# Linear attention, RMS norm and phase token mixing on one core: another token order, packed remainders, and the norm's root on another engine

## The chip, the core and the metric

The kernel runs on one core of a Trainium2 chip. A core has engines that run side by side and wait for each other through semaphores: TensorE (PE; its weight loads are listed apart as PEld), VectorE (DVE), ScalarE (ACT), GpSimd (POOL) and SyncE (SP), which here only issues transfers. In both kernels TensorE writes its results to tiles in the memory PSUM, of which the pool `psA` holds eight. The metric is the time of one execution on the device in microseconds (us), lower is better, as a median of several runs.

## What is computed

Eight batches, eight heads of 64 channels, 576 tokens. Linear attention without softmax is followed by an RMS norm per token and head; the heads side by side give x of 576 x 512 per batch. A phase theta = x·w_theta turns x into two parts, which two token matrices mix over the 576 tokens. A channel product with ReLU ends it.

```python
kv = np.einsum('bhsd,bhse->bhde', k, v)
out = np.einsum('bhsd,bhde->bhse', q, kv)
rms = np.sqrt(np.mean(out * out, axis=-1, keepdims=True) + 1e-06)
x = out / rms * g_norm                   # then (B, S, H*D)
theta = x @ w_theta
zr = x * np.cos(theta)
zi = x * np.sin(theta)
y = np.einsum('ts,bsd->btd', w_tok_r, zr) + np.einsum('ts,bsd->btd', w_tok_i, zi)
u = x + y
result = u + np.maximum(u @ w_ch, 0.0)
```

576 tokens are four tiles of 128 and a remainder of 64. Inputs and output are fp32; after the attention product the kernel works in fp16 with fp32 sums.

## The kernel before

P is 128, C 512, S 576, D 64, NT 5 (token tiles, the last of 64), NKC 4 (channel blocks). Per batch: `attention` loads q, k and v in runs of one token of one head (64 fp32 values, 256 bytes), forms k·v for each pair of heads in fp32 and keeps its two diagonal blocks, transposes q, forms raw = q·kv, and normalises raw tile by tile: squares on ScalarE, sums on VectorE, the power -1/2 on GpSimd (line 186), the product with g_norm (line 190) and with raw (line 197) on VectorE. k is loaded by GpSimd's own queue. `moe_head` transposes x, forms theta, reduces it to one turn (lines 234 to 251), and takes sine and cosine on ScalarE. `moe_mid` mixes over tokens; its output has tokens on the partitions. `moe_tail2` transposes u, multiplies by w_ch and stores. The code is set four columns to the left here; cuts are marked `# ...`.

```python
def attention(b):
    # ...
    for (dst, src, eng) in ((qt, q, nc.sync), (kt, k, nc.gpsimd), (vt, v, nc.sync)):
        for h in range(H):
            eng.dma_start(
                out=dst[:, 0:NT - 1, h, :],
                in_=src[b, h, 0:(NT - 1) * P, :].rearrange(
                    "(sc p) d -> p sc d", p=P
                ),
            )
    # ...
    for hp in range(NHP):
        kvps = psA.tile([P, P], FP32, tag="psA", name=f"kvps{b}_{hp}")
        for sc in range(NT):
            nc.tensor.matmul(
                kvps[:, :],
                kt[:tsz[sc], sc, 2 * hp:2 * hp + 2, :],
                vt[:tsz[sc], sc, 2 * hp:2 * hp + 2, :],
                start=(sc == 0),
                stop=(sc == NT - 1),
            )
        # ...
        nc.vector.memset(kbd[:], 0.0)
        nc.scalar.copy(kbd[0:64, 0:64], kvps[0:64, 0:64])
        nc.scalar.copy(kbd[64:128, 64:128], kvps[64:128, 64:128])
            # ...
            nc.tensor.matmul(
                dst_ap,
                qt[:tsz[sc], sc, 2 * hp:2 * hp + 2, :],
                ident[:tsz[sc], :tsz[sc]],
                is_transpose=True,
                start=(sc in (0, NT - 1)),
            # ...
            )
    # ...
    for ti in range(NT):
        n = tsz[ti]
        raw = psA.tile([P, C], FP32, tag="psA", name=f"raw{b}_{ti}")
        for hp in range(4):
            nc.tensor.matmul(
                raw[:n, hp * P:(hp + 1) * P],
                qT_pair[hp][:, ti * P:ti * P + n],
                kv_bd[hp][:],
                start=(hp == 0),
                stop=(hp == 3),
            )
        # ...
        nc.scalar.activation(out=sq[:n, :], in_=raw[:n, :], func=AFT.Square)
        # ...
        nc.vector.reduce_sum(
            out=sst[:n, :], in_=sq[:n, :].rearrange("p (h e) -> p h e", h=H),
            axis=mybir.AxisListType.X,
        )
        # ...
        nc.gpsimd.tensor_tensor(
            out=rt[:n, :], in0=sse[:n, :], in1=mhalf[:n, 0:H], op=ALU.pow
        )
        # ...
        nc.vector.tensor_tensor(
            out=gr[:n, :].rearrange("p (h e) -> p h e", h=H),
            in0=g_rep[:n, :].unsqueeze(1).broadcast_to((n, H, D)),
            in1=rt[:n, :].unsqueeze(2).broadcast_to((n, H, D)),
            op=ALU.mult,
        )
        # ...
        nc.vector.tensor_tensor(
            out=x16[:n, :], in0=raw[:n, :], in1=gr[:n, :], op=ALU.mult
        )
# ...
def moe_head(b):
    # ...
    for kc in range(NKC):
        xps = psA.tile([P, S], FP16, tag="psA", name=f"xTps{b}_{kc}")
        for ti in range(NT):
            nc.tensor.matmul(
                xps[:, ti * P:ti * P + tsz[ti]],
                xb[ti][:tsz[ti], kc * P:(kc + 1) * P],
                ident16[:tsz[ti], :tsz[ti]],
                is_transpose=True,
            # ...
            )
        # ...
        nc.scalar.copy(out=t[:], in_=xps[:])
    # ...
    for ti in range(NT):
        n = tsz[ti]
        thps = psA.tile([P, C], FP32, tag="psA", name=f"th{b}_{ti}")
        for kc in range(NKC):
            nc.tensor.matmul(
                thps[:n, :],
                xT[kc][:, ti * P:ti * P + n],
                wth_t[kc][:],
                start=(kc == 0),
                stop=(kc == NKC - 1),
            )
        pt = work.tile([P, C], FP32, tag="pt", bufs=3, name=f"pt{b}_{ti}")
        nc.vector.tensor_scalar(
            out=pt[:n, :], in0=thps[:n, :], scalar1=INV2PI, scalar2=MAGIC,
            op0=ALU.mult, op1=ALU.add,
        )
        # ...
        nc.vector.tensor_scalar(
            out=mt[:n, :], in0=pt[:n, :], scalar1=MAGIC, scalar2=TWO_PI,
            op0=ALU.subtract, op1=ALU.mult,
        )
        # ...
        nc.vector.tensor_tensor(
            out=red[:n, :], in0=thps[:n, :], in1=mt[:n, :], op=ALU.subtract
        )
        # ...
        nc.vector.tensor_scalar(
            out=ared[:n, :].bitcast(I32), in0=red[:n, :].bitcast(I32),
            scalar1=0x7FFFFFFF, scalar2=None, op0=ALU.bitwise_and,
        )
        # ...
        nc.scalar.activation(
            out=sin_t[:n, :], in_=red[:n, :], func=AFT.Sin, scale=SIN_SHRINK
        )
        # ...
        nc.scalar.activation(
            out=cos_t[:n, :], in_=ared[:n, :], func=AFT.Sin,
            bias=pio2_t[:n], scale=-SIN_SHRINK,
        )
        # ...
        nc.vector.tensor_tensor(
            out=zrt[:n, :], in0=xb[ti][:n, :], in1=cos_t[:n, :], op=ALU.mult
        )
        # ...
        nc.vector.tensor_tensor(
            out=zit[:n, :], in0=xb[ti][:n, :], in1=sin_t[:n, :], op=ALU.mult
        )
# ...
def moe_mid(b):
    # ...
    for ti in range(NT):
        # ...
        for sc in range(NT):
            for (wT, zz) in ((wrT, zr), (wiT, zi)):
                nc.tensor.matmul(
                    yps[:n, :],
                    wT[sc][:tsz[sc], ti * P:ti * P + n],
                    zz[sc][:tsz[sc], :],
                    start=(i_mm == 0),
                    stop=(i_mm == n_mm - 1),
                )
        # ...
        nc.vector.tensor_tensor(
            out=ut[:n, :], in0=xb[ti][:n, :], in1=yps[:n, :], op=ALU.add
        )
# ...
def moe_tail2(b):
    # ...
    for kc in range(NKC):
        ups = psA.tile([P, S], FP16, tag="psA", name=f"uTps{b}_{kc}")
        for ti in range(NT):
            nc.tensor.matmul(
                ups[:, ti * P:ti * P + tsz[ti]],
                ub[ti][:tsz[ti], kc * P:(kc + 1) * P],
            # ...
            )
        # ...
        nc.scalar.copy(out=t[:], in_=ups[:])
    # ...
    for ti in range(NT):
        # ...
        for kc in range(NKC):
            nc.tensor.matmul(
                vps[:n, :],
                uT[kc][:, ti * P:ti * P + n],
                wch_t[kc][:],
                start=(kc == 0),
                stop=(kc == NKC - 1),
            )
        # ...
        nc.vector.scalar_tensor_tensor(
            out=ot[:n, :], in0=vps[:n, :], scalar=0.0, in1=ub[ti][:n, :],
            op0=ALU.max, op1=ALU.add,
        )
        nc.sync.dma_start(out=out[b, ti * P:ti * P + n, :], in_=ot[:n, :])
# ...
attention(0)
moe_head(0)
for b in range(1, B):
    attention(b)
    moe_mid(b - 1)
    moe_head(b)
    moe_tail2(b - 1)
moe_mid(B - 1)
moe_tail2(B - 1)
```

Ahead of this the weights are loaded: w_theta and w_ch in fp32 with a cast on ScalarE, the token matrices in fp32, transposed on TensorE and cast on the way out of PSUM. The order of instructions on an engine can differ from the program's where they do not depend on each other.

## Time and profile before

| | |
|---|---|
| median of three runs | 407.88 us (404.64 to 407.97) |
| span of the profiled execution | 404.0 us |
| instructions | 5022 |
| bytes read / written | 33.10 MB / 9.44 MB |
| mean granted TensorE clock | 0.916 |

In the lines of the profile, L186 is line 186 of the kernel; out<-in are the names of the tiles (written, then read), x40 the count, then the busy time in us and the mean duration of one in ns, and after a second bar the idle time of the engine just before such instructions, with what ended it. The clock row cuts the span into 40 slices; each digit is the clock granted to TensorE in tenths, 9 being 90% or more. The chain of waits is followed back from the last instruction, each step to what released it.

### The profile page before, as it was taken

The page shows a single profiled execution, that of the slowest core. Times are in us where ns is not written, and L with a number is a line of the kernel's source. Part 1 is how long each engine was busy: PE and PEld are TensorE (multiplying, and loading weights), DVE is VectorE, ACT ScalarE, POOL GpSimd, SP SyncE. Part 2 cuts the span into 40 slices and gives each one's busy share as a digit, 9 for nine tenths or more (in the row PEclk, how much of TensorE's full clock was granted, in tenths as well). Part 3 has the DMA queues.
Part 4 walks back from the last instruction along what each step waited for, and adds up shares of the span by engine and source line. Part 5 has one row for each costly group of instructions (what it writes and reads, how often), then busy time and mean ns, then how long its engine had stood idle before and what let it go on. Part 6 is the DMA issues. An engine that isn't in the chain of part 4 may idle for free.

```text
span 404.0 us, 5022 instructions
## 1 busy us (share of the span) xinstructions
PE 321.1 (79%) x1730; PEld 165.2 (41%) x1730; DVE 235.7 (58%) x515; ACT 156.9 (39%) x342; POOL 120.0 (30%) x120
## 2 busy tenths in 40 slices
PE   0258914997789958996989868995899689978894
PEld 0125701652347323642456324732374235524331
DVE  1000063867695659656694659565875777476953
ACT  2143513470276125540475027612553145503701
POOL 8500292076002920086005710291003400250000
PEclk9999955899699988999899969997999988996998
DMA  7999999069103960289006920398030001200033
GB/s 218 241 242 231 203 222 172 2 135 200 18 0 131 225 113 2 98 175 183 15 34 184 209 44 0 134 218 118 2 114 6 1 0 41 78 0 2 0 118 118
DMA packets 87369, 42.87 MB, mean 106 GB/s; under 512 B 78256, under 2 KB 78256, under 8 KB 87344
## 3 DMA queue, kind: packets, MB, share of 16 engines
q1 hardware_dynamic: 83888, 33.11, 40.0%
q0 software_dynamic: 3456, 9.44, 10.1%
q8 instruction: 14, 0.23, 0.3%
q14 instruction: 11, 0.09, 0.1%
HBM read 33.10 MB, written 9.44 MB: 105 GB/s over the span
## 4 chain that ended last, share of the span: by engine, by line
PE 37%; POOL 20%; DVE 18%; ACT 10%; DMA 7%; issue 5%; POOLq 1%; SPq 0%; DVEq 0%
POOL rt L186 15%; PE kvps L130 11%; PE th L226 9%; POOL k L114 6%; PE v L320 4%; DMA wths<-in_moe_w_theta_dram 4%; PE qTpsa L148 3%; DVE x L197 3%; DVE gr L190 3%; ACT uT L314 3%; ACT sin L253 3%; PE y L284 3%; DVE pt L234 2%; PE xTps L209 2%; ACT cos L257 2%
## 5 line engine op out<-in xcount | busy, mean ns | idle before, releaser
L114 POOL DMA_DIRECT2D k<-in_k_dram x64 | 48.3, 760 | 158.0 <-PE kvps L130 155.3
L186 POOL TENSOR_TENSOR rt<-sse,mhalf 128x8 f32<-128x8 f32 (+1 forms) x40 | 65.3, 1642 | 83.5 <-DVE sse L181 83.3
L284 PE MATMUL y<-zr,wrT 128*128 128x512 f16 (+3 forms) x200 | 76.6, 384 | 1.1 <-DVE x L197 1.1
L284 PE MATMUL y<-zi,wiT 128*128 128x512 f16 (+3 forms) x200 | 75.7, 379 | 0.0
L218 ACT COPY xT<-xTps 128x576 f16<-128x576 f16 x32 | 18.4, 651 | 110.0 <-PE xTps L209 109.8
L209 PE MATMUL xTps<-ident,x 128*128 128x128 f16 (+1 forms) x160 | 19.8, 250 | 41.4 <-DVE x L197 39.8
L130 PE MATMUL kvps<-v,k 128*128 128x128 f32 (+1 forms) x320 | 51.3, 299 | 1.6 <-ACT kvbd L140 1.6
L226 PE MATMUL th<-wth,xT 128*128 128x512 f16 (+1 forms) x160 | 51.4, 490 | 1.1 <-ACT xT L218 1.1
L190 DVE TENSOR_TENSOR gr<-g_rep,rt 128x512 f32<-128x512 f32 (+1 forms) x40 | 27.6, 691 | 41.1 <-POOL rt L186 41.1
L320 PE MATMUL v<-wch,uT 128*128 128x512 f16 (+1 forms) x160 | 41.4, 406 | 8.4 <-ACT uT L314 8.4
L130 PEld LDWEIGHTS kvps<-v,k 128*128 128x128 f32 (+1 forms) x320 | 41.4, 194 | 10.4 <-issue 2.9
L253 ACT ACTIVATE sin<-red 128x512 f16<-128x512 f32 (+1 forms) x40 | 25.2, 631 | 51.0 <-DVE red L244 51.0
L234 DVE TENSOR_SCALAR pt<-th 128x512 f32<-128x512 f32 (+1 forms) x40 | 26.6, 683 | 29.9 <-PE th L226 29.9
L138 DVE MEMSET kvbd<- 128x64 uint32 x32 | 3.1, 112 | 62.1 <-ACT qT L158 48.0
L284 PEld LDWEIGHTS <-wrT 128*128 128x128 f16 (+3 forms) x200 | 19.7, 98 | 44.3 <-issue 27.9
L209 PEld LDWEIGHTS <-x 128*128 128x128 f16 (+1 forms) x160 | 11.6, 109 | 51.5 <-DVE x L197 44.2
L328 DVE SCALAR_TENSOR_TENSOR ot<-v,u 128x512 f32<-128x512 f32 (+1 forms) x40 | 26.1, 679 | 9.9 <-DMA out_dram<-ot 6.8
L176 DVE TENSOR_REDUCE sst<-sq 128x8 f32<-128x512 f16 (+1 forms) x40 | 26.1, 679 | 8.4 <-ACT sq L174 8.0
L226 PEld LDWEIGHTS <-xT 128*128 128x128 f16 (+1 forms) x160 | 18.4, 123 | 31.0 <-issue 20.0
L257 ACT ACTIVATE cos<-ared,pio_t 128x512 f16<-128x512 f32 (+1 forms) x40 | 28.6, 718 | 0.7 <-DVE ared L248 0.4
L293 DVE TENSOR_TENSOR u<-x,y 128x512 f16<-128x512 f16 (+1 forms) x40 | 26.1, 672 | 3.5 <-PE y L284 3.4
L320 PEld LDWEIGHTS <-uT 128*128 128x128 f16 (+1 forms) x160 | 14.5, 105 | 31.9 <-ACT uT L314 15.6
(48 smaller groups left out, 367.2 us busy)
## 6 DMA issues: line engine op xcount, KB each, us to landing
k<-in_k_dram POOLq DMA_DIRECT2D x72, 128.0 KB, 5.8
q<-in_q_dram SPq DMA_DIRECT2D x72, 128.0 KB, 5.3
v<-in_v_dram SPq DMA_DIRECT2D x72, 128.0 KB, 4.9
out_dram<-ot SPq DMA_DIRECT2D x32, 256.0 KB, 2.0
wrnat<-in_moe_w_tok_r_dram SPq DMA_DIRECT2D x4, 288.0 KB, 7.4
winat<-in_moe_w_tok_i_dram SPq DMA_DIRECT2D x4, 288.0 KB, 4.0
wths<-in_moe_w_theta_dram SPq DMA_DIRECT2D x4, 256.0 KB, 7.0
wchs<-in_moe_w_ch_dram SPq DMA_DIRECT2D x4, 256.0 KB, 4.9
```

Source lines behind the costliest of these rows:

```text
L114: eng.dma_start(out=dst[:, 0:NT - 1, h, :], in_=src[b, h, 0:(NT - 1) * P, :].rearrange("(sc p) d -> p sc d", p=P),)
L130: nc.tensor.matmul(kvps[:, :], kt[:tsz[sc], sc, 2 * hp:2 * hp + 2, :], vt[:tsz[sc], sc, 2 * hp:2 * hp + 2, :], start=(sc == 0), stop=(sc = ...
L176: nc.vector.reduce_sum(out=sst[:n, :], in_=sq[:n, :].rearrange("p (h e) -> p h e", h=H), axis=mybir.AxisListType.X,)
L186: nc.gpsimd.tensor_tensor(out=rt[:n, :], in0=sse[:n, :], in1=mhalf[:n, 0:H], op=ALU.pow)
L190: nc.vector.tensor_tensor(out=gr[:n, :].rearrange("p (h e) -> p h e", h=H), in0=g_rep[:n, :].unsqueeze(1).broadcast_to((n, H, D)), in1=rt[ ...
L209: nc.tensor.matmul(xps[:, ti * P:ti * P + tsz[ti]], xb[ti][:tsz[ti], kc * P:(kc + 1) * P], ident16[:tsz[ti], :tsz[ti]], is_transpose=True, ...
L226: nc.tensor.matmul(thps[:n, :], xT[kc][:, ti * P:ti * P + n], wth_t[kc][:], start=(kc == 0), stop=(kc == NKC - 1),)
L234: nc.vector.tensor_scalar(out=pt[:n, :], in0=thps[:n, :], scalar1=INV2PI, scalar2=MAGIC, op0=ALU.mult, op1=ALU.add,)
L253: nc.scalar.activation(out=sin_t[:n, :], in_=red[:n, :], func=AFT.Sin, scale=SIN_SHRINK)
L257: nc.scalar.activation(out=cos_t[:n, :], in_=ared[:n, :], func=AFT.Sin, bias=pio2_t[:n], scale=-SIN_SHRINK,)
L284: nc.tensor.matmul(yps[:n, :], wT[sc][:tsz[sc], ti * P:ti * P + n], zz[sc][:tsz[sc], :], start=(i_mm == 0), stop=(i_mm == n_mm - 1),)
L320: nc.tensor.matmul(vps[:n, :], uT[kc][:, ti * P:ti * P + n], wch_t[kc][:], start=(kc == 0), stop=(kc == NKC - 1),)
```

## The change

The kernel is written anew around the same mathematics.

- **Token order.** Within the first 512 tokens, partition p now holds the tokens 4p to 4p+3, so that a load moves runs of 1 KB, and a store row of the output stays 2 KB. k and q are regrouped on GpSimd into tiles by head pair (`ks`, `qs`; q to fp16). All loads of q, k and v go by SyncE's queue.
- **Packed remainders.** The 64 remaining tokens are laid out twice, on both halves of a 128-row tile. One half becomes the cosine part and the other the sine part, so that the mix has nine full contraction blocks instead of ten of which two have 64 rows.
- **Mix transposed.** The mix takes z as the stationary operand, and its output has channels on the partitions, which is what the channel product needs; u is transposed back for the last addition.
- **Norm.** The sums of squares of all five tiles are collected, and the inverse square root is a first guess from the bits and two Newton steps on VectorE. g_norm times the root of D is a value per partition, applied where x is transposed and where the mix is read out.
- **Phase.** theta comes in eighths of a turn (the factor is in w_theta's cast), rounding is an addition on ScalarE, one VectorE instruction gives the fraction.
- **Weights.** The token matrices and w_ch are loaded by GpSimd's queue with a cast to fp16.

The diff takes out all of the code above and is set four columns to the left, like it. What it puts in its place, with the set-up of constants and tiles, w_theta's load and some closing lines cut:

```diff
-def attention(b):
-def moe_head(b):
-def moe_mid(b):
-def moe_tail2(b):
+def load(b, pieces):
+    # ...
+    for h in range(0, H, step):
+        for (dst, last, src, eng) in (
+            (kt, kl, k, nc.sync), (vt, vl, v, nc.sync), (qt, ql, q, nc.sync)
+        ):
+            eng.dma_start(
+                out=dst[:, h:h + step, :, :].rearrange("p h j d -> p h (j d)"),
+                in_=src[b, h:h + step, 0:SF, :].rearrange(
+                    "h (p j) d -> p h (j d)", j=NF
+                ),
+            )
+# ...
+def token_weights():
+        # ...
+        for tj in range(NT):
+            # ...
+            nc.tensor.matmul(
+                pw[:, tj * P:tj * P + rows], st, ident16[:rows, :rows],
+                is_transpose=True, start=(tj == 0), stop=(tj == NT - 1),
+            )
+# ...
+def rsqrt(y, s, tmp):
+    nc.vector.tensor_scalar(
+        out=y.bitcast(I32), in0=s.bitcast(I32), scalar1=-0.5,
+        scalar2=float(0x5F3759DF), op0=ALU.mult, op1=ALU.add,
+    )
+    for _ in range(2):
+        nc.vector.scalar_tensor_tensor(
+            out=tmp, in0=y, scalar=-0.5, in1=y, op0=ALU.mult, op1=ALU.mult
+        )
+        nc.vector.tensor_tensor(out=tmp, in0=tmp, in1=s, op=ALU.mult)
+        nc.vector.scalar_tensor_tensor(
+            out=y, in0=tmp, scalar=1.5, in1=y, op0=ALU.add, op1=ALU.mult
+        )
+# ...
+def attention_kq(b):
+    # ...
+    for hp in range(HP):
+        pair = slice(2 * hp, 2 * hp + 2)
+        ks = work.tile([P, NF, 2, D], FP32, tag="ks", bufs=4, name=f"ks{b}_{hp}")
+        nc.gpsimd.tensor_copy(ks[:].rearrange("p j h d -> p h j d"), kt[:, pair, :, :])
+        qs = work.tile([P, NT, 2, D], FP16, tag="qs", bufs=4, name=f"qs{b}_{hp}")
+        nc.gpsimd.tensor_copy(
+            qs[:, 0:NF].rearrange("p j h d -> p h j d"), qt[:, pair, :, :]
+        )
+        nc.gpsimd.tensor_copy(qs[:T, NF], ql[:, pair, :])
+        for j in range(NT):
+            lhs = ks[:, j, :, :] if j < NF else kl[:, pair, :]
+            rhs = vt[:, pair, j, :] if j < NF else vl[:, pair, :]
+            nc.tensor.matmul(
+                kvp[:, hp, :], lhs, rhs, start=(j == 0), stop=(j == NT - 1)
+            )
+        pq = ps([P, SX], FP16, f"qTps{b}_{hp}")
+        for (j, rows, at) in blocks:
+            nc.tensor.matmul(
+                pq[:, at:at + rows], qs[:rows, j, :, :], ident16[:rows, :rows],
+                is_transpose=True, start=(at == 0), stop=(at + rows == SX),
+            )
+        t = work.tile([P, SX], FP16, tag="qT", bufs=2 * HP, name=f"qT{b}_{hp}")
+        nc.scalar.copy(out=t[:], in_=pq[:])
+        qT.append(t)
+    bd = kv_bd[b % 2]
+    for r in range(2):
+        nc.scalar.copy(
+            out=bd[r * D:(r + 1) * D, :, r * D:(r + 1) * D],
+            in_=kvp[r * D:(r + 1) * D, :, r * D:(r + 1) * D],
+        )
+# ...
+def attention_x(b):
+    # ...
+    for ti in range(NT):
+        raw = ps([P, C], FP32, f"raw{b}_{ti}")
+        for hp in range(HP):
+            nc.tensor.matmul(
+                raw[:, hp * P:(hp + 1) * P], qT[hp][:, ti * P:(ti + 1) * P], bd[:, hp, :],
+                start=(hp == 0), stop=(hp == HP - 1),
+            )
+        sq = work.tile([P, C], FP32, tag="sq", bufs=3, name=f"sq{b}_{ti}")
+        nc.scalar.activation(out=sq[:], in_=raw[:], func=AFT.Square)
+        nc.vector.reduce_sum(
+            out=ss[:, ti, :], in_=sq[:].rearrange("p (h e) -> p h e", h=H),
+            axis=mybir.AxisListType.X,
+        )
+        raws.append(raw)
+    nc.vector.tensor_scalar(
+        out=ss[:], in0=ss[:], scalar1=D * eps, scalar2=None, op0=ALU.add
+    )
+    rsqrt(rt[:], ss[:], tm[:])
+    for ti in range(NT):
+        raw = raws[ti]
+        xt = work.tile([P, C], FP16, tag="x", bufs=2 * NT, name=f"x{b}_{ti}")
+        nc.vector.tensor_tensor(
+            out=xt[:].rearrange("p (h e) -> p h e", h=H),
+            in0=raw[:].rearrange("p (h e) -> p h e", h=H),
+            in1=rt[:, ti, :].unsqueeze(2).broadcast_to((P, H, D)),
+            op=ALU.mult,
+        )
+# ...
+def phase(b):
+    # ...
+    for kc in range(NK):
+        px = ps([P, SX], FP16, f"xTps{b}_{kc}")
+        for (ti, rows, at) in blocks:
+            nc.tensor.matmul(
+                px[:, at:at + rows], x[ti][:rows, kc * P:(kc + 1) * P],
+                ident16[:rows, :rows],
+                is_transpose=True, start=(at == 0), stop=(at + rows == SX),
+            )
+        nc.scalar.activation(
+            out=xT[:, kc, :], in_=px[:], func=AFT.Copy, scale=gcol[:]
+        )
+    # ...
+    for ti in range(NT):
+        th = ps([P, C], FP32, f"th{b}_{ti}")
+        for kc in range(NK):
+            nc.tensor.matmul(
+                th[:], xT[:, kc, ti * P:(ti + 1) * P], wth[:, kc, :],
+                start=(kc == 0), stop=(kc == NK - 1),
+            )
+        # ...
+        nc.scalar.activation(
+            out=pt[:], in_=th[:], func=AFT.Identity, bias=magic_t[:]
+        )
+        # ...
+        nc.vector.scalar_tensor_tensor(
+            out=f[:], in0=pt[:], scalar=MAGIC, in1=th[:],
+            op0=ALU.subtract, op1=ALU.subtract,
+        )
+        if ti < NF:
+            # ...
+            nc.vector.tensor_scalar(
+                out=fa[:].bitcast(I32), in0=f[:].bitcast(I32),
+                scalar1=0x7FFFFFFF, scalar2=None, op0=ALU.bitwise_and,
+            )
+            for (n, src, bias) in ((ti, fa, pio2_t), (NF + ti, f, None)):
+                # ...
+                nc.scalar.activation(
+                    out=tr[:], in_=src[:], func=AFT.Sin, scale=-RAD,
+                    **({"bias": bias[:]} if bias is not None else {}),
+                )
+                zt = work.tile([P, C], FP16, tag=f"z{n}", bufs=2, name=f"z{b}_{n}")
+                nc.vector.tensor_tensor(out=zt[:], in0=x[ti][:], in1=tr[:], op=ALU.mult)
+        # ...
+        else:
+            # ...
+            nc.scalar.activation(
+                out=tr[:], in_=f[:], func=AFT.Sin, scale=-RAD, bias=tail_bias[:]
+            )
+            # ...
+            nc.vector.tensor_tensor(out=zt[:], in0=x[ti][:], in1=tr[:], op=ALU.mult)
+# ...
+def mix(b):
+    # ...
+    yl = ps([P, NK, T], FP32, f"yl{b}")
+    for kc in range(NK):
+        y = ps([P, SF], FP32, f"y{b}_{kc}")
+        for n in range(2 * NF + 1):
+            lhs = z[n][:, kc * P:(kc + 1) * P]
+            nc.tensor.matmul(
+                y[:], lhs, wT[n][:, 0:SF], start=(n == 0), stop=(n == 2 * NF)
+            )
+            nc.tensor.matmul(
+                yl[:, kc, :], lhs, wT[n][:, SF:S], start=(n == 0), stop=(n == 2 * NF)
+            )
+        for (o, yy, n) in ((0, y[:], SF), (SF, yl[:, kc, :], T)):
+            nc.vector.scalar_tensor_tensor(
+                out=uT[:, kc, o:o + n], in0=yy, scalar=gcol[:],
+                in1=xT[:, kc, o:o + n], op0=ALU.mult, op1=ALU.add,
+            )
+# ...
+def channel(b):
+    # ...
+    for ti in range(NT):
+        # ...
+        pu = ps([P, C], FP16, f"ups{b}_{ti}")
+        for kc in range(NK):
+            nc.tensor.matmul(
+                pu[:rows, kc * P:(kc + 1) * P], uT[:, kc, ti * P:ti * P + rows],
+                ident16[:], is_transpose=True, start=(kc == 0), stop=(kc == NK - 1),
+            )
+        # ...
+        nc.scalar.copy(out=u[:rows], in_=pu[:rows])
+        # ...
+        for kc in range(NK):
+            nc.tensor.matmul(
+                vp[:rows], uT[:, kc, ti * P:ti * P + rows], wch[:, kc, :],
+                start=(kc == 0), stop=(kc == NK - 1),
+            )
+        # ...
+        nc.vector.scalar_tensor_tensor(
+            out=ot[:rows], in0=vp[:rows], scalar=0.0, in1=u[:rows],
+            op0=ALU.max, op1=ALU.add,
+        )
+# ...
+attention_kq(0)
+attention_x(0)
+# ...
+for (i, src) in ((0, moe_w_tok_r), (1, moe_w_tok_i)):
+    nc.gpsimd.dma_start(
+        out=wnat[i][:], in_=src[0:SF, :].rearrange("(p j) s -> p j s", j=NF)
+    )
+    nc.gpsimd.dma_start(out=wnatl[i][:], in_=src[SF:S, :])
+    nc.gpsimd.tensor_copy(wtt[:, 0:NF, i, :], wnat[i][:, :, SF:S])
+    nc.gpsimd.tensor_copy(wtt[:T, NF, i, :], wnatl[i][:, SF:S])
+wch = wpool.tile([P, NK, C], FP16, tag="wch", name="wch")
+nc.gpsimd.dma_start(out=wch[:], in_=moe_w_ch.rearrange("(k p) c -> p k c", p=P))
+load(1, 1)
+phase(0)
+token_weights()
+for b in range(B):
+    if b + 1 < B:
+        attention_kq(b + 1)
+        if b + 2 < B:
+            load(b + 2, 1)
+    if b > 0:
+        channel(b - 1)
+    if b + 1 < B:
+        attention_x(b + 1)
+    mix(b)
+    if b + 1 < B:
+        phase(b + 1)
+channel(B - 1)
```

NF is 4 (full tiles), SF 512, T 64, SX 640, NK 4, HP 4; `blocks` lists the four full tiles and the remainder twice.

## The prediction

> **What bounds the kernel now.** I read the page first: shares of busy time and the clock row.
>
> ```profile
> PE 321.1 (79%) x1730; PEld 165.2 (41%) x1730; DVE 235.7 (58%) x515; ACT 156.9 (39%) x342; POOL 120.0 (30%) x120
> ...
> PEclk9999955899699988999899969997999988996998
> ```
>
> No engine is full, and the granted clock dips once per batch. So next comes the chain of waits over one batch (columns: start us, length us, what).
>
> ```profile
> 216.01 0.80 POOL k L114
> ...
> 217.12 2.27 POOL k L114 x4
> ...
> 220.10 3.27 POOL rt L186 x2
> 223.36 0.75 POOL k L114
> 224.12 1.49 POOL k L114 x2
> ...
> 226.32 3.28 POOL rt L186 x2
> ...
> 231.73 1.63 POOL rt L186
> 233.39 0.68 DVE gr L190
> ...
> 235.33 1.38 PE xTps L209 x9
> 236.71 3.79 PE th L226 x9
> ```
>
> From 216 to 233 us the chain lies on GpSimd: five inverse square roots of 1.63 us, one per token tile, and between them the issues of the next k load, 0.75 us each. Only then can x be formed and transposed. The same th row begins at 148.98 and 366.97 us in the whole chain: five batches in 218.0 us, so a batch takes 43.6 us. The table by stage shows what TensorE does meanwhile (columns after the window: its length, then busy us of PE, PEld, DVE, ACT, POOL, clock, DMA share, GB/s).
>
> ```profile
> 217.70:229.60 11.90, 11.90 (x53) 4.17 (x50) 7.47 (x17) 2.42 (x5) 11.85 (x12) 1.00 1.19 225
> 229.60:235.30 5.70, 1.17 (x12) 0.66 (x11) 4.46 (x9) 0.00 (x0) 1.63 (x1) 0.83 1.10 168
> 236.60:243.00 6.40, 6.40 (x23) 2.39 (x23) 2.49 (x7) 1.26 (x3) 0.00 (x0) 0.72 0.01 3
> 247.00:253.00 6.00, 6.00 (x32) 3.16 (x30) 5.71 (x14) 3.91 (x8) 0.00 (x0) 1.00 0.00 0
> ```
>
> The token mix (first row) hides the root chain for 11.9 us; then TensorE works 1.17 of 5.70 us, and the theta product after it runs at clock 0.72: 6.34 us for 20 matmuls. Adding the pieces of one batch in the timeline: k·v with q transposes 4 x 2.30 = 9.2, raw 1.4, y 11.9, xT 1.4, th 6.3, uT 1.9, v 18 in 4.18, so 4.6 for 20; together 36.7. The other 6.9 us are gaps. Batch 0's th starts only at 67.75 us.
>
> **What the Trainium skill says.** "TensorE: Matmul & The Clock Gate", Part 1, says that an idle array falls to half clock and regains it after about 3.4 us of sustained work. The 0.72 above agrees. "ScalarE: Activation LUTs", What ACT_TABLE_LOAD costs, puts a per-partition pointer operand at about 93 ns more. Here cos, with one, and sin, without:
>
> ```profile
> L257 ACT ACTIVATE cos<-ared,pio_t 128x512 f16<-128x512 f32 x32 | 22.9, 718 | 0.4
> L253 ACT ACTIVATE sin<-red 128x512 f16<-128x512 f32 x32 | 20.2, 632 | 51.0 <-DVE red L244 51.0
> ```
>
> That is 86 ns, so it agrees. "GPSIMD Engine Reference", Performance versus the Vector engine, gives 769 ns for a loop[...] over 512 elements; no copy of this size by GpSimd is in this trace, so that stays an estimate. "DMA: Bandwidth & Descriptors", Specifications, wants at least 512 B per piece. The trace counts 78256 packets under 512 B, and the windows agree in direction: 330 GB/s while weight rows of 2 KB move with them, 211 with q, k, v alone.
>
> ```profile
> 6.00:10.00 4.00, 0.92 (x2) 0.36 (x2) 0.00 (x0) 0.93 (x2) 3.16 (x5) 1.00 1.05 330
> 54.00:60.00 6.00, 1.21 (x8) 0.69 (x8) 3.44 (x10) 0.00 (x0) 5.98 (x7) 0.50 1.26 211
> ```
>
> **The change, part by part: TensorE per batch.** k·v keeps its fp32 operands: 10 pieces in 1.50, 4 x 1.50 = 6.0 us. q's transposes become six in fp16; uTps did 20 in 1.92, 0.096 each, so 24 x 0.096 = 2.3 (before 3.2). raw is unchanged, 1.4. xT has 24 transposes, 2.3. th is 20 x 0.215 = 4.3 at full clock (0.215 is the start-to-start step of y matmuls). The mix changes most: four channel blocks with nine contraction blocks each, because the two 64-row remainders are packed into one block of 128. That is 36 matmuls of 512 columns and 36 of 64. A raw matmul of 128 columns steps at 1.41/20 = 0.070 us; I take 0.065 for 64 columns. 36 x (0.215 + 0.065) = 10.1 against 11.9. Transposing u back: 20 x 0.070 = 1.4. v stays 4.6. Sum 6.0 + 2.3 + 1.4 + 2.3 + 4.3 + 10.1 + 1.4 + 4.6 = 32.4 us.
>
> **VectorE per batch**, rows with PSUM at 0.68, fp16 or SBUF-only at 0.42: sums of squares 5, x 5, fraction 5, output 5: 20 x 0.68 = 13.6; the mix's eviction 4 x (0.68 + 0.2) = 3.5; absolute value 5 and z 9: 14 x 0.42 = 5.9; the root as eight small operations of about 0.2 = 1.6. Sum 24.6. gr, the second rounding step and the memsets are gone. **ScalarE**: qT 4 x 0.70 (576 columns took 0.65), kv blocks 0.8, squares 5 x 0.60, xT 4 x 0.80 with a pointer, rounding 5 x 0.69, sines 5 x 0.72 + 4 x 0.63, u 5 x 0.59: 22.3 us. **GpSimd**: eight copies of 512 elements at 0.77 plus four small ones of 0.3 = 7.4 us (before five roots, 8.2, plus 6.8 of k issues), and none of it lies between raw and x.
>
> **What lies on the path.** Between raw and the transposes of x now stand five reductions (3.3, overlapped starts), the root (1.6) and five products (3.0): about 8 us with the first square, beside a mix of 10.1 us. So I take the wait as hidden, the clock as full, and TensorE as the bound. I add 1.5 us per batch for hand-overs (xT eviction, raw's five of eight PSUM tiles held until x, so that the third y block may wait). A batch: about 34 us.
>
> **Start and end.** q, k, v of batch 0 are 3.5 MB; with w_theta, the token weights, w_ch and batch 1 together 11.8 MB. In 1 KB pieces I assume 280 GB/s, between the two windows above: 42 us for all. Batch 0's share comes first but has company from the weights, so complete at about 22 us; copies and k·v 3, raw to x 9, xT 3, theta to z (ScalarE 2 us per tile, five tiles) 10: the first mix starts near 47 us, with batch 1's k·v already done beside it. From there TensorE has 8 mixes 81, 8 channel steps 48, 7 phases 46, 6 k·v steps 50 and 6 raws 8: 233. Hand-overs 7 x 1.5 = 10; the last stores 6 (now 404 - 396 = 8). 47 + 233 + 10 + 6 = 296 us.
>
> **The rivals.**
> (1) The VectorE chain takes the place of GpSimd's. Against: 8 is under 10. For: x now waits for all five tiles, and the previous batch's outputs (5 x 0.68) stand before it on VectorE. If 3 us come late, the clock falls as well: 3 + 2 per batch, times 7, gives about 330.
> (2) GpSimd's copies become the bound. For: its root needs 1.63 us for 8 elements, and the copies regroup runs of 64 elements. At 4 us per copy, 8 x 4 + 4 = 36 us would exceed TensorE: 320 to 340. Against: the root is a different operation, and the estimate leaves a factor of four.
> (3) The start is the transfers' alone: token weights issued on GpSimd compete with batch 0 or wait behind its copies. First mix at 60 instead of 47: about 309. No loss per batch, as 4.7 MB in 34 us need 139 GB/s.
> (4) The shorter side: 64-column matmuls hide almost free and the first mix comes at 40: 8 x 1.3 + 7 less, about 279.
>
> **Range and chances.** The sum says 296; rivals 4 and 3 give 279 and 309, and part of 1 or 2 takes it to 325. I take 274 to 325. Even the bad cases stay far under 408: all of them would have to come together to lose the 112 us. Faster by over 2%: 0.96; within: 0.02; slower: 0.02.
>
> **What would show it.** TensorE's share should rise above 85% and its clock row have no dip per batch after the start; the chain should be mostly PE, with no GpSimd row inside a batch; y should take near 10 us per batch; GpSimd's copies near 0.8 us each; the first mix near 47 us; the period between equal th rows near 34 us. I am wrong if that period is over 37 (a new wait: see who ends the idle time before xTps and the first y) or if GpSimd's copies take 3 us or more.

## The result, and the profile after

| | before | after |
|---|---|---|
| median, us | 405.41 (402.83 to 408.45, 15 runs) | 296.72 (295.44 to 297.82, 12 runs) |
| ratio, 95% interval | 1 | 0.732 [0.729, 0.734] |
| span of the profiled execution, us | 404.0 | 294.3 |
| mean granted clock | 0.916 | 0.970 |

First the page of the changed kernel: busy shares, the clock row, and the shares of the chain that ended last.

```profile
PE 260.2 (88%) x1965; PEld 160.2 (54%) x1965; DVE 192.1 (65%) x412; ACT 164.2 (56%) x283; POOL 59.0 (20%) x111
...
PEclk9999999558999999999999999999999999999999
...
PE 51%; DVE 18%; ACT 13%; DMA 11%; issue 2%; SPq 2%; POOL 1%; DVEq 0%; ACTq 0%
```

TensorE went from 79% to 88% of a shorter span. The dips once per batch are gone; one is left, between 51 and 74 us. GpSimd has 1% of the chain. In the table by stage two batches, the second without GpSimd's copies as no batch is left to prepare (window, length, then busy us of PE, PEld, DVE, ACT, POOL, clock, DMA share, GB/s) look like this:

```profile
172.62:203.50 30.88, 29.75 (x242) 17.98 (x240) 24.45 (x50) 19.43 (x35) 7.34 (x12) 1.00 0.27 82
234.34:264.62 30.28, 29.57 (x241) 18.00 (x240) 22.30 (x50) 19.61 (x35) 0.00 (x0) 1.00 0.12 40
```

A batch takes 30.9 us instead of 43.6 (the mean over six is 43.7), and TensorE is idle for 1.1 us of it instead of 5.4 (mean over the same six). The chain through the end of such a batch (start us, length us, what):

```profile
193.10 2.37 DVE ss L219 x4
195.47 0.67 DVE uT L322
...
196.18 0.59 PE y L315 x2
...
200.75 1.23 PE xTps L249 x18
...
202.00 0.80 ACT xT L254
```

The root, at 196 to 198.5 us, isn't in it: the chain passes from an eviction of u to the mix and straight on to the transposes of x. But VectorE is in it just ahead, with sums of squares and an eviction, so the two are close to each other. How close, the experiments show.

**Where the 110 us of span come from.** Taking theta of batch 1 and theta of batch 7 as marks, the span falls into three parts. The middle column is the experiment "one batched root" below, the kernel before with nothing changed but the root, moved to VectorE and done once per batch. The marks are these rows of the three chains, in the order of the columns:

```profile
104.54 7.52 PE th L226 x20
366.97 3.30 PE th L226 x8
```

```profile
97.33 6.29 PE th L240 x20
323.78 2.14 PE th L240 x9
```

```profile
78.78 4.35 PE th L262 x20
264.62 1.81 PE th L262 x8
```

| us | before | before, one batched root | after |
|---|---|---|---|
| start to theta of batch 1 | 104.5 | 97.3 | 78.8 |
| six batches | 262.4 | 226.5 | 185.8 |
| theta of batch 7 to the end | 37.0 | 35.6 | 29.7 |
| span | 404.0 | 359.4 | 294.3 |

### The profile page after: what moved, and what is told of

It is laid out like the page before. It is cut to its first block, busy times and chain, and to the rows that moved or that the text cites. A ratio compares the mean times of both kernels' runs of the same rounds, so it can differ in the third digit from the quotient of the medians.

```text
span 294.3 us, 5134 instructions
## 1 busy us (share of the span) xinstructions
PE 260.2 (88%) x1965; PEld 160.2 (54%) x1965; DVE 192.1 (65%) x412; ACT 164.2 (56%) x283; POOL 59.0 (20%) x111
## 4 chain that ended last, share of the span: by engine, by line
PE 51%; DVE 18%; ACT 13%; DMA 11%; issue 2%; SPq 2%; POOL 1%; DVEq 0%; ACTq 0%
PE y L315 14%; PE kv L183 10%; PE th L262 9%; PE vps L342 7%; DVE ss L219 4%; ACT tr L283 3%; DVE z L288 3%; DMA out_dram<-ot 3%; PE qTps L188 3%; DVE ot L347 3%; PE xTps L249 3%; DMA v<-in_v_dram 3%; DMA wnat<-in_moe_w_tok_i_dram 3%; DMA k<-in_k_dram 3%; DVE f L271 3%; DVE fa L277 2%
## 5 line engine op out<-in xcount | busy, mean ns | idle before, releaser
L315 PE MATMUL y<-wT,z 128*128 128x512 f16 x256 | 65.1, 380 | 1.7 <-DVE uT L322 1.5
L183 PE MATMUL kv<-v,ks 128*128 128x128 f32 x256 | 43.7, 323 | 11.3 <-DMA v<-in_v_dram 10.9
L183 PEld LDWEIGHTS kv<-v,ks 128*128 128x128 f32 x256 | 38.0, 225 | 13.7 <-issue 11.3
L219 DVE TENSOR_REDUCE ss<-sq 128x8 f32<-128x512 f32 x40 | 24.9, 673 | 28.5 <-ACT sq L218 28.5
L262 PE MATMUL th<-wth,xT 128*128 128x512 f16 x160 | 38.6, 390 | 4.2 <-ACT xT L254 4.1
L342 PE MATMUL vps<-wch,uT 128*128 128x512 f16 (+1 forms) x160 | 41.2, 379 | 1.2 <-ACT u L339 1.2
L271 DVE SCALAR_TENSOR_TENSOR f<-pt,th 128x512 f32<-128x512 f32 x40 | 26.5, 680 | 22.2 <-ACT pt L267 22.2
L347 DVE SCALAR_TENSOR_TENSOR ot<-vps,u 128x512 f32<-128x512 f32 (+1 forms) x40 | 26.0, 683 | 18.9 <-ACT u L339 14.2
L193 ACT COPY qT<-qTps 128x640 f16<-128x640 f16 x32 | 20.8, 684 | 25.7 <-PE qTps L188 25.7
L288 DVE TENSOR_TENSOR z<-x,tr 128x512 f16<-128x512 f16 x64 | 31.9, 525 | 1.2 <-ACT tr L283 1.1
L267 ACT ACTIVATE pt<-th,magic_t 128x512 f32<-128x512 f32 x40 | 24.6, 686 | 5.2 <-PE th L262 5.2
L231 DVE TENSOR_TENSOR x<-raw,rt 128x512 f16<-128x512 f32 x40 | 24.7, 682 | 0.3
```

The lines of the kernel that those rows point to most:

```text
L183: nc.tensor.matmul(kvp[:, hp, :], lhs, rhs, start=(j == 0), stop=(j == NT - 1))
L219: nc.vector.reduce_sum(out=ss[:, ti, :], in_=sq[:].rearrange("p (h e) -> p h e", h=H), axis=mybir.AxisListType.X,)
L231: nc.vector.tensor_tensor(out=xt[:].rearrange("p (h e) -> p h e", h=H), in0=raw[:].rearrange("p (h e) -> p h e", h=H), in1=rt[:, ti, :].un ...
L262: nc.tensor.matmul(th[:], xT[:, kc, ti * P:(ti + 1) * P], wth[:, kc, :], start=(kc == 0), stop=(kc == NK - 1),)
L267: nc.scalar.activation(out=pt[:], in_=th[:], func=AFT.Identity, bias=magic_t[:])
L271: nc.vector.scalar_tensor_tensor(out=f[:], in0=pt[:], scalar=MAGIC, in1=th[:], op0=ALU.subtract, op1=ALU.subtract,)
```

## The experiments

**1. The root leaves GpSimd, and nothing else.** The kernel before, its power -1/2 replaced tile by tile by the changed kernel's arithmetic on VectorE.

```diff
-            nc.gpsimd.tensor_tensor(
-                out=rt[:n, :], in0=sse[:n, :], in1=mhalf[:n, 0:H], op=ALU.pow
-            )
+            nc.vector.tensor_scalar(  # first guess from the bits
+                out=rt[:n, :].bitcast(I32), in0=sse[:n, :].bitcast(I32), scalar1=-0.5,
+                scalar2=float(0x5F3759DF), op0=ALU.mult, op1=ALU.add,
+            )
+            # ... and two Newton steps of three small operations, as in rsqrt
```

> The kernel before with one part of the change: the inverse square root leaves GpSimd and becomes seven small operations per token tile on VectorE (guess from the bits, two Newton steps). Theory (the GpSimd chain of roots and k issues makes the gap before xTps): x no longer waits for GpSimd, the 6.9 us of gaps per batch shrink to about 2 and th runs at full clock; a batch goes from 43.6 to about 37 us, the time to about 360. Rival (VectorE takes the chain over): 5 x 7 operations of about 0.2 us add 7 us to VectorE's 29.4 per batch, which is then 36 us and in order; the batch stays above 41, the time above 390.

Measured: 406.58 us, ratio 1.000 [0.996, 1.004]: no change, as the rival had it. In the chain of this kernel VectorE now fills the place of GpSimd's rows (start us, length us, what), and the timeline of TensorE's transposes of x still shows idle time before them (last, in brackets, with what ended it):

```profile
223.75 0.08 DVE sse L181
223.83 0.59 DVE x L211
224.42 0.60 DVE gr L204
225.02 0.08 DVE rt L187
```

```profile
230.61 0.40 PE L223 MATMUL xTps<-ident,x 128*128 128x128 f16 x4 [0.82 <-DVE x L211]
231.94 0.40 PE L223 MATMUL xTps<-ident,x 128*128 128x128 f16 x4 [0.93 <-DVE tm L192]
234.40 0.29 PE L223 MATMUL xTps<-ident,x 64*128 64x64 f16 x4 [2.06 <-DVE x L211]
```

Five times over, a tile's sum, eight small operations, gr and x stand in one engine's queue, mixed with u, which waits for y. The mix ends at 229.2, and TensorE is then idle for 3.8 us in three pieces, where the kernel before had 4.6. So "the chain lies on GpSimd" was true of the profile, and yet GpSimd alone was not the cause.

**2. k's issues leave GpSimd, and nothing else.** The kernel before with `(kt, k, nc.gpsimd)` turned into `(kt, k, nc.sync)`.

> The kernel before with another part alone: k is loaded by SyncE's queue, so that GpSimd does only the roots. Theory (half of the chain is the k issues that stand between the roots): the chain from raw to the last x shortens by about 5 us, from 17 to about 12, which the mix of 11.9 us just covers; a batch takes 38 to 39 us, the time about 370. Rival (the roots alone hold it, 5 x 1.63 plus hand-overs): the gap before xTps stays above 3 us, the time above 395.

Measured: 399.41 us, ratio 0.983 [0.977, 0.990]: 7 us by the ratio, of some 108. TensorE still waits for 4.1 us before the transposes of x in such a batch, as the rival expected.

**3. One batched root.** The kernel before; the sums of the five tiles go into one tile, then eight operations on 128 x 40 on VectorE, then the five products.

```diff
-                out=sst[:n, :], in_=sq[:n, :].rearrange("p (h e) -> p h e", h=H),
+                out=ss[:n, ti, :], in_=sq[:n, :].rearrange("p (h e) -> p h e", h=H),
 # ...
+            raws.append(raw)
+        # the added epsilon, the guess and two Newton steps, once on ss, into rt
+        for ti in range(NT):
+            n = tsz[ti]
+            raw = raws[ti]
-                in1=rt[:n, :].unsqueeze(2).broadcast_to((n, H, D)),
+                in1=rt[:n, ti, :].unsqueeze(2).broadcast_to((n, H, D)),
```

> The kernel before with the changed kernel's way of the root: sums of all five tiles first, then one root of 128x40 on VectorE in eight operations, then the products. Theory (with the root per tile on VectorE some 40 small operations took GpSimd's place in VectorE's sequence between raw and x): 32 of them go, the stretch shortens by about 4 us, a batch goes from 43.6 to 40, the time to 380. Rival (VectorE's 20 large operations between raw and the last x, with the u sums among them, fill the mix's 11.9 us by themselves and raw's PSUM tiles delay the mix): 400 or more.

Measured: 361.42 us, ratio 0.895 [0.889, 0.900]. Its clock row, and from TensorE's timeline the only transposes of x that wait in this batch:

```profile
PEclk9999995799989999999999999999999999999998
```

```profile
248.37 0.29 PE L223 MATMUL xTps<-ident,x 64*128 64x64 f16 x4 [0.54 <-DVE x L211]
```

The mix ends at 246.8, and TensorE is idle for 0.5 us instead of experiment 1's 3.8. Both have the root on VectorE; they differ in five rounds or one, and with it in the number of small operations: VectorE is busy for 242.6 us here and for 260.7 there. Less work is not the whole reason, since the kernel before, with 235.7 us on VectorE and the root on GpSimd, was as slow as experiment 1. With the gaps this short the clock row has hardly a dip after the start, and that is much of the gain: TensorE's own busy time falls from 321.1 us to 300.3, 20.8 of the 44.6 us of span. A batch is 37.7 us: 34.9 of TensorE work, 2.8 idle.

**4. The batched root goes back to GpSimd.** The changed kernel, `rsqrt` replaced by one power of 128 x 40 on GpSimd.

```diff
-        rsqrt(rt[:], ss[:], tm[:])
+        nc.gpsimd.tensor_tensor(
+            out=rt[:].rearrange("p t h -> p (t h)"), in0=ss[:].rearrange("p t h -> p (t h)"),
+            in1=mhalf[:], op=ALU.pow,
+        )
```

> The changed kernel with one part undone: the root of all five tiles is one power instruction of 128x40 on GpSimd. Theory (the root is hidden beside the mix and TensorE is the bound): up to 3 us more from raw to x cost nothing; with 1.6 us for 8 columns, 40 columns take between 1.6 and 8.2 us, so the time stays within 2% if the instruction takes under 4 us, and rises to about 330 if it takes 8. Rival (any lengthening of the chain raw to x shows at once, because the mix waits for PSUM tiles that raw holds): plus the whole difference, 7 x (instruction - 1.6).

Measured: 348.94 us, ratio 0.859 [0.853, 0.864]. The row of the power, among one tile's instructions (shortest, median and longest ns), and a row of the list of TensorE's waits (us in total, times, longest):

```profile
L226 POOL TENSOR_TENSOR rt<-ss,mhalf x8: 6760/6761/6801, 32.4 to 301.6; 128x40 f32<-128x40 f32 x8
```

```profile
PE y L317 <- DVE x L233: 36.2, 7, 5.4
```

Five times the elements take 6.76 us instead of 1.63, against 8.15 for five single ones, so batching on GpSimd saves little. The root is 5.2 us longer than on VectorE, and a batch 6.5 (52 over eight), so nothing of it is hidden. The excess goes with the clock: its row dips once per batch again, and TensorE's own busy time grows from 260.2 to 275.3 us. And it isn't the transposes of x that wait, but y: its third block needs a PSUM tile, and five of the eight are held by raw until x is formed.

**5. The mix without most of its narrow matmuls.** The changed kernel; the 64-column matmul is issued for `n == 0` alone, so the last 64 tokens' sum over the other blocks is left out.

```diff
-                nc.tensor.matmul(
-                    yl[:, kc, :], lhs, wT[n][:, SF:S], start=(n == 0), stop=(n == 2 * NF)
-                )
+                if n == 0:
+                    nc.tensor.matmul(
+                        yl[:, kc, :], lhs, wT[n][:, SF:S], start=True, stop=True
+                    )
```

> The changed kernel without 32 of the 36 matmuls of 64 columns in each mix (only the first contraction block of the 64 remaining tokens is computed; 256 matmuls are left out in all). Theory: with the weights already in place such a matmul adds 0.03 us (a pair steps at 0.245, a single one of 512 columns at 0.215), so 7.7 us fewer than the changed kernel's 296.7: about 289. Rival, the prediction's own figure: 0.065 us each, 16.6 us fewer: about 280. Second rival: the mix doesn't set the time, since x and the third output block wait for the norm beside it: under 3 us, 294 or more.

Measured: 307.15 us, ratio 0.756 [0.748, 0.763]: slower with less work, which no theory expected; only the second rival's "294 or more" covers it. The mix in TensorE's timeline of this kernel (start, length, then in brackets the idle time before and what ended it):

```profile
163.65 1.89 PE L315 MATMUL y<-wT,z 128*128 128x512 f16 x8
...
166.11 0.19 PE L319 MATMUL yl<-wT,z 128*128 128x64 f16 x1 [0.35 <-DVE ot L348]
167.20 1.89 PE L315 MATMUL y<-wT,z 128*128 128x512 f16 x8 [0.91 <-DVE ot L348]
```

The mix lasts from 163.7 to 173.1, 9.4 us, as long as in the changed kernel (191.3 to 200.6): what TensorE no longer computes, it waits, here for PSUM tiles that the previous batch's outputs hold on VectorE; one of these outputs itself waited 0.41 us for a store. After the mix the transposes of x wait as well, and a batch takes 32.2 us (mean of six). The program's order of VectorE's instructions came out differently too; how the extra 1.3 us per batch divides between that and the lost work stays open.

**6. The narrow matmuls twice as wide.** The changed kernel; 128 columns instead of 64, half of them not read. VectorE's order is nearly that of the changed kernel.

```diff
-        yl = ps([P, NK, T], FP32, f"yl{b}")
+        yl = ps([P, NK, 2 * T], FP32, f"yl{b}")
-                    yl[:, kc, :], lhs, wT[n][:, SF:S], start=(n == 0), stop=(n == 2 * NF)
+                    yl[:, kc, :], lhs, wT[n][:, SF - T:S], start=(n == 0), stop=(n == 2 * NF)
-            for (o, yy, n) in ((0, y[:], SF), (SF, yl[:, kc, :], T)):
+            for (o, yy, n) in ((0, y[:], SF), (SF, yl[:, kc, T:], T)):
```

> The changed kernel with each of the mix's narrow matmuls made 128 columns wide instead of 64 (the other 64 columns are computed once more and not read). Theory, TensorE sets the batch: a column costs about 0.0004 us (0.215 us for 512 columns less 0.034 for 64, over 448), so 64 more columns cost 0.026 us, 36 of them 0.93 us per batch, eight batches 7.4 us: about 304. Rival, VectorE's way from raw to x ends at the same time or later, as the run without the narrow matmuls suggests: the addition is hidden, under 2 us, 296 to 299.

Measured: 300.58 us, ratio 0.744 [0.741, 0.748], 3.9 us over the changed kernel: between the two theories. The direct cost is read where eight narrow ones run in a row, first in the changed kernel, then in this one:

```profile
203.07 0.40 PE L318 MATMUL yl<-wT,z 128*128 128x64 f16 x8
```

```profile
176.34 0.62 PE L318 MATMUL yl<-wT,z 128*128 128x128 f16 x8
```

The length of a row is seven steps and one whole matmul (0.19 and 0.22 by the rows of one): steps of 0.030 and 0.057 us. 288 x 0.027 = 7.8 us of TensorE work were added, and only some of it shows: half by the medians, 5 us by the ratios. TensorE and VectorE end the stage together: here TensorE leaves the mix at 174.5 and x is complete at 175.1, in the changed kernel at 200.6 and 201.6.

**7. k and v in fp16 for k·v, copied by GpSimd.** The changed kernel; `ks` becomes fp16, `vs` is a new regrouped fp16 copy of v.

```diff
-            ks = work.tile([P, NF, 2, D], FP32, tag="ks", bufs=4, name=f"ks{b}_{hp}")
+            ks = work.tile([P, NT, 2, D], FP16, tag="ks", bufs=4, name=f"ks{b}_{hp}")
+            vs = work.tile([P, NT, 2, D], FP16, tag="vs", bufs=4, name=f"vs{b}_{hp}")
+            # ... filled by nc.gpsimd.tensor_copy like qs, and used in the matmul
```

> The changed kernel with less work for TensorE alone: k and v are copied to fp16 by GpSimd, so that a head pair needs 5 pieces of about 0.07 us in place of 10 pieces in 1.50. Theory (TensorE is the bound): 4 x 1.15 = 4.6 us less per batch on TensorE, up to 36 us in all, about 262 if nothing else limits; VectorE, busy 24.4 us per batch, is next, so between 262 and 275. Rival (the exchange between VectorE, ScalarE and PSUM tiles sets the batch already): less than 2%, 292 to 300. Second rival (the extra copies on GpSimd, about 5 us per batch, slow VectorE): 280 to 292.

Measured: 302.06 us, ratio 0.742 [0.738, 0.747]: slower than with fp32. Two batches of this kernel, from theta to theta, one with the next batch's copies, and one without:

```profile
140.10:174.24 34.14, 29.41 (x221) 15.47 (x221) 26.91 (x50) 19.56 (x35) 12.12 (x24) 0.90 0.45 139
242.27:270.86 28.59, 26.34 (x221) 14.36 (x220) 22.11 (x50) 19.21 (x35) 0.00 (x0) 1.00 0.13 43
```

The absolute value, in the changed kernel and here (shortest, median, longest ns):

```profile
L277 DVE TENSOR_SCALAR fa<-f x32: 419/421/836, 44.2 to 272.7; 128x512 int32<-128x512 int32 x32
```

```profile
L286 DVE TENSOR_SCALAR fa<-f x32: 414/421/2112, 41.8 to 279.0; 128x512 int32<-128x512 int32 x32
```

Without copies beside it a batch takes 28.6 us, where the changed kernel takes 30.3: less work for TensorE does help. With them it takes 34.1, as the absolute value and z are stretched up to five times on VectorE while GpSimd copies. That is the second rival's cause, with a larger cost than it gave. "GPSIMD Engine Reference", Specifications, says that GpSimd's SBUF interfaces are shared with VectorE, with contention for instructions in a two-port mode or with two SBUF inputs; these rows agree: z has two inputs in SBUF, and the absolute value takes 0.42 us where the sum of squares takes 0.68 for as many elements, so I take it to be in a faster mode. The absolute value and z come in the phase, where a chain of VectorE and ScalarE feeds the mix, and there the clock dipped to 0.90.

**8. GpSimd's copies, more of them.** The changed kernel with two more copies of k per head pair into a tile that nobody reads.

```diff
+            for i in range(2):
+                k2 = work.tile([P, NF, 2, D], FP32, tag="k2", bufs=1, name=f"k2{b}_{hp}{i}")
+                nc.gpsimd.tensor_copy(k2[:].rearrange("p j h d -> p h j d"), kt[:, pair, :, :])
```

> The changed kernel with more work for GpSimd alone: two further copies of k per head pair into a tile that nobody reads, 8 x 0.73 = 5.8 us per batch. Theory (GpSimd's copies slow VectorE's SBUF operations, and VectorE's sequence is tight with TensorE's): VectorE's z and absolute-value rows lengthen again, a batch goes from 30.9 to about 33 us, the time to about 310. Rival (TensorE alone bounds, VectorE has 6 us to spare): within 1%, 294 to 300.

Measured: 301.21 us, ratio 0.745 [0.741, 0.748]. The 4.5 us lie at the start (theta of batch 1 at 84.0 us instead of 78.8). Two rows of the chain there, the first two operations of batch 0's root, which take 0.17 us each when no copy runs beside them:

```profile
30.21 3.45 DVE ss L227
33.68 0.65 DVE rt L152
```

A batch in the middle is unchanged:

```profile
147.56:178.45 30.89, 29.75 (x241) 18.00 (x240) 24.43 (x50) 19.44 (x35) 12.67 (x21) 1.00 0.50 154
```

GpSimd is busy 5.3 us longer, and VectorE not at all: the extra copies fell beside other operations. So it's not the amount of copying that costs, but what it meets: the absolute value and z in experiment 7, and here, at the start, the root.

**9. k·v of batch 1 ahead of the token weights.** The changed kernel with the calls in another order.

```diff
     phase(0)
+    attention_kq(1)
     token_weights()
     for b in range(B):
         if b + 1 < B:
-            attention_kq(b + 1)
+            if b > 0:
+                attention_kq(b + 1)
```

> The changed kernel with one line moved: batch 1's k·v and q transposes come before the transposes of the token weights. Theory (the late start is an order of work: TensorE waits for the token weights at 47 to 51 us, falls to half clock and then does batch 1's k·v in 13.5 us while z of batch 0, ready at 53.5, waits): TensorE does k·v at full clock from 44 to 52, the token weights after it, and the first mix starts near 58 in place of 67.7; the time falls by 8 to 10 us, to about 287. Rival (the first mix is late because of the transfers): same time, 295 to 299.

Measured: 286.69 us, ratio 0.709 [0.705, 0.713]: 10 us less, and the clock row has no dip left. The first mix starts at 57.5 us, as expected.

**10. The same, with four output tiles instead of three** (`bufs=4` for `ot`).

> The changed kernel with k·v of batch 1 ahead of the token weights (286.69 us so far) and four output tiles instead of three. Theory: the waits of outputs for stores are some 3% of the chain and one more tile hides little of them: within 1% of 286.7. Rival: the stores do hold the channel stage in every batch; 4 to 6 us less, 281 to 283.

Measured: 283.18 us, ratio 0.699 [0.694, 0.704]. Nearer to the rival: the outputs did wait for stores, and that is worth 3.5 us, as they stand ahead of the sums of squares on VectorE. A batch of it:

```profile
132.11:162.34 30.23, 30.15 (x240) 18.05 (x240) 24.37 (x50) 19.42 (x35) 7.34 (x12) 1.00 0.50 157
```

TensorE is idle for less than 0.1 us, VectorE is gone from the chain of this batch, and it is 0.7 us shorter than in experiment 9 (30.9). So what TensorE waited for in the changed kernel's batches was mostly outputs that waited for stores, with the work that stands behind them on VectorE.

**11. Loads that cast.** The changed kernel; from batch 1 on k, v and q are loaded straight into the regrouped layout in fp16, by GpSimd's queue, in pieces of 256 bytes of the source. GpSimd copies nothing for these batches, and k·v is in fp16. The issues for these batches:

```diff
+                for h in range(H):
+                    nc.gpsimd.dma_start(
+                        out=t16[:, 0:NF, h, :],
+                        in_=src[b, h, 0:SF, :].rearrange("(p j) d -> p j d", j=NF),
+                    )
```

> The changed kernel with k, v and q in fp16, loaded from batch 1 on by GpSimd's queue with a cast, into the layout that TensorE needs, in runs of 256 bytes; GpSimd copies only batch 0. Theory (the copies on GpSimd slowed VectorE in the run with fp16 copies; without them TensorE's 25 us and VectorE's 22 us per batch count): a batch takes 28.6 us, as the last batches of that run, and the time is about 283. Rival (27 issues of 0.76 us per batch on GpSimd and the short runs delay the loads): no better than 297. Third possibility: the writing of descriptors slows VectorE as the copies did, about 300.

Measured: 282.7 us, ratio 0.699 [0.693, 0.706]: 13 to 14 us under the changed kernel, near the theory's 283. (Two of its four runs were in the slower of two states that executions of a kernel show; time and ratio are of the other two.) GpSimd's issues don't stretch z, which stays within 0.409 to 0.427 us, so the third possibility is out. What still held it back is read from the next one.

**12. Loads that cast, the other order, and eight output tiles.**

> The changed kernel with three edits together: from batch 1 on, k, v and q are cast to fp16 by the load itself (so no GpSimd copies and k·v in fp16), k·v of batch 1 is placed ahead of the token weights, and the output tile has eight buffers instead of three. Theory: the casting loads alone gave batches of 30 to 32 us while loads ran and 28.6 without them, because VectorE's outputs waited for slow stores to free their tile; with eight tiles they no longer wait, so all batches come near 28.6, and the other order takes 10 us off the start: 268 to 272 us. Rival: the loads in 256-byte pieces hold the stores and themselves back whatever the number of tiles; batches stay at 30 to 32 and only the start's 10 us, or part of them, is won: 275 to 285.

Measured: 269.23 us, ratio 0.665 [0.661, 0.669], the fastest version here, a third under the kernel before. A batch of it:

```profile
154.34:182.24 27.90, 26.56 (x220) 14.43 (x221) 22.18 (x50) 19.46 (x35) 18.04 (x25) 1.00 1.05 101
```

The theory held: 27.9 us with loads under way. Against experiment 11 it is 13.4 us; the order is worth 9 to 10 of them by experiment 9, so by difference the output tiles are worth some 4, near the 3.5 of experiment 10; with casting loads they weren't tried alone. GpSimd is busy with issues for 18 us and DMA is at 1.05, and neither is in the chain of this batch, which runs mainly through ScalarE and VectorE: TensorE is no longer the only bound.

## Why the prediction was right

The time was within 1 us of the predicted 296. Its parts weren't that close: the first mix came 21 us later than predicted, what follows it took 22 us less, and the two cancel.

- **The bound.** TensorE at full clock, "a batch: about 34 us". It is 30.9, with 29.7 of work and 1.1 idle. The mechanism was right, and the clock too.
- **The terms of the sum.** Predicted 32.4, measured 29.7 of work. k·v and q 7.9 (8.3 predicted), theta 4.3 (4.3), u back and v 5.7 (6.0), raw 1.2 (1.4), transposes of x 1.6 (2.3), mix 8.8 (10.1). The term that was most off is the 64-column matmul, "I take 0.065": it adds 0.030; 36 x 0.035 = 1.3 us per batch. Taking nearly raw's 128-column step of 0.070 for it was the slip: the two rows in experiment 6 step at 0.057 with 128 columns and at 0.030 with 64, so the step follows the columns. That each follows a matmul with the same stationary block isn't the reason: the trace of the changed kernel lists a weight load for each of them (the first of two such rows is below), and in the row of experiment 6 eight with eight different blocks step at 0.030 as well. "TensorE: Matmul & The Clock Gate", Back-to-back issue gap, has a formula, columns / 2.4 + 2.5 ns, that gives 0.029, 0.056 and for 512 columns 0.216; here 0.030, 0.057 and 0.215 were measured. The sustained figure that it sets beside the formula for 512 columns, 0.131, isn't what these runs show.

```profile
L318 PEld LDWEIGHTS <-z 128*128 128x128 f16 x256 | 14.8, 98 | 8.4 <-issue 2.8
```

- **The other operands.** GpSimd's copies take 0.73 us for k, against 0.77 estimated; VectorE is busy 24.45 us per batch against 24.6; ScalarE 19.4 against 22.3. Rival 2 is out.
- **"So I take the wait as hidden."** True, but only just. In experiment 4 none of 5.2 us more is hidden, and in 5 and 6 the mix doesn't follow TensorE's work: the way from raw to x ends with it. Rival 1 is what stands right behind, and experiment 10 shows what brought it so close: outputs that wait for stores. With a fourth output tile the batch is all TensorE.
- **The start, "the first mix starts near 47 us ... with batch 1's k·v already done beside it": this step failed.** The first y is at 67.7 us. The chain there, of the changed kernel:

```profile
38.44 5.76 PE th L262 x20
...
50.70 0.52 PE wTps L138 x5
...
51.57 2.77 PE kv L183 x10
...
65.64 2.29 PE raw L213 x20
```

x of batch 0 is done at 37.2 (34 was predicted) and its z at 53.5 (47). Then k·v of batch 1 isn't done: it begins at 51.6, right after the transposes of the token weights, which stand ahead of it in the program. It also runs at half clock, 10 pieces in 2.7 us instead of 1.50, after TensorE had worked for only 2.99 of the 5 us from 45 to 50. These 14 us and raw's 2.3 lie on the path. Experiment 9 takes 10 us of it away by order alone. Rival 3 named the right place, but the transfers aren't the whole reason.
- **What made the gain.** The prediction put the gap on GpSimd's roots and issues. Experiments 1 to 3 divide this: moving the root saves 0 us, the issues 7, the root moved and batched 44.6 by the spans. GpSimd filled the chain in the kernel before, VectorE in experiment 1, where the same five rounds passed through it: this step of the prediction had the wrong reason. The other 65 us lie in the remaining parts, k's issues among them: by the table above 41 in six batches (34.9 to 29.7 us of TensorE work in each, and idle time from 2.8 to 1.1), 18.5 at the start, 6 at the end. These parts weren't tried one by one.

## What to carry to other kernels

An engine that fills the chain of waits may be there because of the form of the work, several short rounds through three engines, and not because it is slow: move the work without changing its form before you believe it. Where two engines end a stage within a microsecond of each other, work taken off one of them can show up as waiting, as in experiment 5, so look for buffers held across the stage (PSUM tiles kept by raw, output tiles kept by stores) as well as for busy time. A time that comes out right says little about its terms; compare the marks inside the span, first of all the first use of the steady stage.

## What the runs showed of the hardware

- **GpSimd's copies stretch some of VectorE's operations, and not others.** The absolute value and z go from 0.42 us up to 0.87 in the changed kernel and 2.11 in experiment 7; the addition of epsilon, on 40 elements, from 0.17 to 3.44 in experiment 8. The sum of squares, with one input in SBUF, stays within 0.666 to 0.689 in the first two, the fraction, x and the outputs, which read PSUM, within 0.670 to 0.693, and the eviction of u within 0.730 to 0.752.
- **A power on GpSimd has hardly a fixed cost to share.** 1.63 us for 8 elements per partition, 6.76 for 40: 5.13 us for 32 more, 0.16 each, which leaves some 0.35 us of the 1.63 that doesn't grow. Eight VectorE operations on the same 40 take 0.17 to 0.20 each.
- **The clock row can read full where TensorE isn't.** At 10.9 to 24 us of the changed kernel ten k·v pieces take 2.7 us, as at half clock later (2.7), while the row reads 9. The record seems to begin with its first change; that is an inference from the step of the matmuls.
